# Eight V heads as a 512-wide moving operand, and single rows of 512 for an MLP and an output projection, in a one-token attention kernel

## The chip, the cores and the metric

The kernel runs on one core of one Trainium2 chip. The metric is device time in microseconds (us), the median of several executions of the same program. Five engines work side by side, each in its own program order: PE (TensorE, matrix products), DVE (VectorE), ACT (ScalarE), POOL (GpSimd) and SP, which here only issues the loads. Sixteen DMA engines move the data. In the profile, PEld are PE's weight loads and PEclk is the share of full clock that PE was granted. A line such as `L283` names a line of the kernel's source; the source of the changed kernel has other line numbers.

## The reference

One token decodes through attention over the last 4,096 positions of a cache with 32 heads, and through a small MLP on the same normalised input; the results are multiplied and added to the input. Cut to what matters:

```python
xn = _layernorm(x)                              # x is (1, 1, 512)
q  = xn @ wq                                    # 32 heads of 128
k, v = k_cache[:, :, Sk - W:], v_cache[:, :, Sk - W:]   # W = 4096
scores = einsum("bhqd,bhkd->bhqk", q, k) * Dh ** -0.5
o  = einsum("bhqk,bhkd->bhqd", softmax(scores), v)
s  = o.reshape(B, Sq, 4096) @ wo                # back to 512
# MLP; its shifts leave zeros for a sequence of one token
x1 = xn + hs                                    # hs = shifted @ w2
g  = silu(x1 + gelu(layernorm(x1) @ w3) @ w4)
out = x + s * g
```

Nearly all data are the 32 K and 32 V heads, 1 MB each, every byte used once.

## The kernel before

K and V heads arrive in order through one queue, V five heads behind K. Heads with an even number get their scores on DVE: a multiplication with q (about 2.3 us) and a reduction (4.4 us). Heads with an odd number get them on PE: 32 transposes of 128 x 128, four copies by ACT, and 32 narrow matmuls with q. Four heads share a softmax.

```python
def k_head(h, kn):
    ...
    if h % 2 == 0:                        # DVE
        nc.vector.tensor_tensor(out=prod[:], in0=kn[:], in1=q_bc[...], op=ALU.mult)
        nc.vector.tensor_reduce(out=s["sS"][:, hl // 2, :], in_=prod[:], axis=AX.X, op=ALU.add)
    else:                                 # PE and ACT
        for b in range(NB):
            for i in range(8):
                nc.tensor.transpose(pt[:, i, :], kn[:, b * 8 + i, :], ident_bf[:])
            nc.scalar.copy(out=kt[:, b * 8:(b + 1) * 8, :], in_=pt[:])
    ...
    if hl == G - 1:
        softmax(g)                        # maxima, exponentials: PE, DVE, ACT in turn
```

A V head is used as the stationary operand, 32 weight loads with a matmul of one column after each. The products with the output weights wo, and those of the MLP, go four at a time into rows 0, 32, 64 and 96 of a PSUM tile, 128 wide each:

```python
def rows_add(ps, col, w, last):
    k = col.shape[0]
    for j in range(KC):                   # KC = 4
        nc.tensor.matmul(ps[32 * j:32 * j + 1, :], lhsT=col, rhs=w[0:k, j * P:(j + 1) * P],
                         start=False, stop=last, skip_group_check=True)

def apply_wo(i, ox):                      # once per block of 8 heads
    for t in range(8):
        rows_add(y_ps, ox[:, t:t + 1], wo_blk[i][:, t, :], False)

def v_head(h, v):
    ...
    for c in range(NC):                   # NC = 32
        nc.tensor.matmul(oT[:, k:k + 1], lhsT=v[:, c, :], rhs=s["pT"][:, hl % 2, hl // 2, c:c + 1],
                         start=(c == 0), stop=(c == NC - 1))
    ...                                   # after head 7, 15, 23 and 27:
            ox = repack(i)                # DVE, PE, DVE, DVE
            later.append(lambda: apply_wo(i, ox))
```

The loop `for i in range(H + LAG)` calls `k_head(i)` and then `v_head(i - 5)`. "K27" below is K head 27, "V31" V head 31, the last one. "wo block 0, 1, 2" are the products of heads 0 to 7, 8 to 15 and 16 to 23; the last eight heads have a path of their own, which the change leaves alone.

## Time and profile before

| Kernel before | |
|---|---|
| Time, median of 3 | 197.74 us (197.67 to 197.79) |
| Span of the profiled run | 195.5 us |
| Mean clock granted to PE | 0.649 |
| Last V landed on the first of its DMA engines, on the last | 185.80, 190.54 us |
| PE begins on the last V | 190.58 us, after 1.31 us of waiting |

The prediction below quotes the slices, the waits of the queue and the end of the chain. Three more places matter for what came. The first is part 4 of the page of before, the composition of the chain that ended last:

```profile
DMA 57%; PE 18%; DVE 16%; issue 3%; ACT 3%; SPq 1%; DVEq 0%; ACTq 0%
```

More than half of that chain is transfers: again and again an engine waited for data. The second place is PE's timeline of before from 140 to 156 us. Columns are start, duration, engine, line, operation, output and inputs, shapes and count; in brackets stands the idle time ahead and what ended it.

```profile
140.50 1.03 PE L402 MATMUL oT<-pT,kv 128*128 128x1 bf16 x32
141.87 3.59 PE L283 MATMUL pt<-ident_bf,kv 128*128 128x128 bf16 x32 [0.33 <-DMA kv<-in_A_k_cache_dram]
145.25 0.61 PE L255 MATMUL sT<-qT_bf,kt 128*128 128x1 bf16 x16
146.89 0.99 PE L402 MATMUL oT<-pT,kv 128*128 128x1 bf16 x32 [1.03 <-DVE o L409]
...
149.58 1.01 PE L402 MATMUL oT<-pT,kv 128*128 128x1 bf16 x32 [1.27 <-DMA kv<-in_A_v_cache_dram]
151.99 3.60 PE L283 MATMUL pt<-ident_bf,kv 128*128 128x128 bf16 x32 [1.39 <-DMA kv<-in_A_k_cache_dram]
```

K25 (141.87), a V head and K27 (151.99) all waited for DMA: PE has caught up with the data here. The waits for data add up to 0.33 + 1.27 + 1.39 = 3.0 us. The third place is the same view some 10 us on:

```profile
160.32 1.03 PE L402 MATMUL oT<-pT,kv 128*128 128x1 bf16 x32
166.97 0.21 PE L363 MATMUL ox_ps<-spread,to 128*128 128x64 bf16 x1 [5.61 <-DVE spread L360]
167.79 1.02 PE L139 MATMUL y_ps<-wo,ox 128*1 128x128 bf16 x32 [0.62 <-DVE ox L369]
168.75 2.96 PE L283 MATMUL pt<-ident_bf,kv 128*128 128x128 bf16 x32
```

PE is idle for 5.61 us, the largest gap of the stretch. But this gap doesn't wait for data: it waits for DVE, which stands behind the multiplication and reduction of K28, which stand behind the softmax of heads 24 to 27, which needs the scores of K27. Such a gap moves with K27.

### The profile page before, as it was taken

Reading aid. Unit: us, or ns where it says so; the run is one execution under the profiler, and the core shown is the slowest. Engines: PE = TensorE matmul, PEld = TensorE weight load, DVE = VectorE, ACT = ScalarE, POOL = GpSimd, SP = SyncE. Lnnn points to the kernel's source line nnn. Section 1 sums busy time; section 2 is a strip of 40 time slices with the busy share of each in tenths; the row PEclk is TensorE's granted clock in tenths of the full one; section 3 lists DMA queues with packets and bytes.
Section 4 is the critical chain, followed back from the end, with each engine's and each line's share of the span. In section 5 each row is a group of like instructions: output and inputs, shape, how many; then the busy total and the mean of one; then the engine's idle time right before and its main releaser. Section 6 shows DMA issues by size and latency. Waiting matters only on the chain.

```text
span 195.5 us, 5353 instructions
## 1 busy us (share of the span) xinstructions
PE 125.0 (64%) x2448; PEld 113.4 (58%) x2448; DVE 129.6 (66%) x165; ACT 69.3 (35%) x82; POOL 5.8 (3%) x12
## 2 busy tenths in 40 slices
PE   0564496827969693099783772399584950798663
PEld 0463346827959683099683662299484950687552
DVE  1530059998979988985199919694699559691501
ACT  2003038709345270055453250077170610257000
POOL 2110007000000000000000000000000000000000
PEclk9999999675585555555558585576555555588555
DMA  6999899999999999999999999999999999999970
GB/s 209 409 496 426 372 424 419 424 426 417 426 424 426 426 424 422 422 427 427 422 424 427 422 424 422 427 426 422 422 427 424 424 422 427 429 424 417 418 292 8
DMA packets 11518, 79.18 MB, mean 405 GB/s; under 512 B 1384, under 2 KB 2248, under 8 KB 2504
## 3 DMA queue, kind: packets, MB, share of 16 engines
q1 hardware_dynamic: 11344, 78.85, 96.4%
q8 instruction: 19, 0.31, 0.6%
q10 hardware_dynamic: 152, 0.00, 0.0%
q14 instruction: 3, 0.02, 0.0%
HBM read 78.84 MB, written 0.00 MB: 403 GB/s over the span
## 4 chain that ended last, share of the span: by engine, by line
DMA 57%; PE 18%; DVE 16%; issue 3%; ACT 3%; SPq 1%; DVEq 0%; ACTq 0%
DMA kv<-in_A_v_cache_dram 30%; DMA kv<-in_A_k_cache_dram 18%; DMA wq_sb<-in_A_wq_dram 10%; DVE sS L277 7%; PE pt L283 7%; DVE prod L274 6%; PE oT L402 4%; PE sT L255 2%; ACT kt L284 2%; SPq L76 1%; PE mb_ps L307 1%; PE qT_ps L225 1%; PE qb_ps L234 1%; PE y_ps L139 1%; PE mt_ps L300 1%
## 5 line engine op out<-in xcount | busy, mean ns | idle before, releaser
L284 ACT COPY kt<-pt 128x1024 bf16<-128x1024 bf16 x64 | 60.2, 1026 | 68.2 <-PE pt L283 68.2
L277 DVE TENSOR_REDUCE sS<-prod 128x32 f32<-128x4096 bf16 x16 | 70.6, 4414 | 0.3
L283 PE MATMUL pt<-ident_bf,kv 128*128 128x128 bf16 x512 | 53.4, 298 | 3.4 <-DMA kv<-in_A_k_cache_dram 3.2
L283 PEld LDWEIGHTS <-kv 128*128 128x128 bf16 x512 | 49.8, 141 | 4.7 <-DMA kv<-in_A_k_cache_dram 3.4
L274 DVE TENSOR_TENSOR prod<-kv,q_bc 128x4096 bf16<-128x4096 bf16 x16 | 36.6, 2285 | 6.3 <-DMA kv<-in_A_k_cache_dram 4.1
L402 PEld LDWEIGHTS <-kv 128*128 128x128 bf16 x1024 | 30.6, 102 | 16.5 <-issue 10.0
L402 PE MATMUL oT<-pT,kv 128*128 128x1 bf16 x1024 | 32.6, 165 | 8.3 <-DVE o L409 4.2
L255 PE MATMUL sT<-qT_bf,kt 128*128 128x1 bf16 x512 | 20.4, 166 | 3.5 <-ACT kt L284 3.1
L255 PEld LDWEIGHTS <-kt 128*128 128x128 bf16 x512 | 18.2, 103 | 4.5 <-ACT kt L284 4.2
L297 DVE TENSOR_REDUCE m<-sT 128x2 f32<-128x64 f32 x8 | 1.8, 224 | 19.3 <-PE sT L255 19.3
L139 PEld LDWEIGHTS <-ox 128*1 128x1 bf16 x96 | 2.2, 114 | 19.5 <-DVE ox L369 19.5
L363 PE MATMUL ox_ps<-spread,to 128*128 128x64 bf16 x4 | 0.8, 212 | 17.4 <-DVE spread L360 17.4
L316 ACT ACTIVATE pT<-e 128x128 bf16<-128x128 f32 x8 | 2.5, 310 | 20.7 <-DVE e L312 20.7
L307 PEld LDWEIGHTS mb_ps<-md,ones_f 4*128 4x128 f32 x16 | 3.8, 290 | 6.1 <-DVE md L304 6.1
L307 PE MATMUL mb_ps<-md,ones_f 4*128 4x4 f32 x16 | 4.5, 347 | 4.4 <-DVE md L304 4.4
L322 PE MATMUL den_ps<-pT,ones_bf 128*128 128x128 bf16 x8 | 2.1, 265 | 7.3 <-ACT pT L316 7.2
L300 PE MATMUL mt_ps<-ident_f,m 128*4 128x128 f32 x8 | 2.7, 334 | 5.9 <-DVE m L297 5.9
L236 ACT CAST q_bc<-qb_ps 128x512 bf16<-128x512 f32 x4 | 2.3, 586 | 9.9 <-PE qb_ps L234 9.9
L234 PE MATMUL qb_ps<-wq_sb,xn_rep 128*128 128x512 bf16 x16 | 5.3, 506 | 0.0
L225 PE MATMUL qT_ps<-xn_bf,wq_sb 128*128 128x1 bf16 x64 | 1.9, 165 | 5.2 <-DMA wq_sb<-in_A_wq_dram 5.2
L225 PEld LDWEIGHTS <-wq_sb 128*128 128x128 bf16 x64 | 1.8, 104 | 5.5 <-DMA wq_sb<-in_A_wq_dram 5.5
L309 DVE COPY mb<-mb_ps 128x4 f32<-128x4 f32 x8 | 1.3, 163 | 5.3 <-PE mb_ps L307 5.3
(96 smaller groups left out, 61.6 us busy)
## 6 DMA issues: line engine op xcount, KB each, us to landing
kv<-in_A_k_cache_dram SPq DMA_DIRECT2D x32, 1024.0 KB, 19.6
kv<-in_A_v_cache_dram SPq DMA_DIRECT2D x32, 1024.0 KB, 19.6
wq_sb<-in_A_wq_dram SPq DMA_DIRECT2D x1, 4096.0 KB, 18.9
wo<-in_A_wo_dram SPq DMA_DIRECT2D x3, 1024.0 KB, 20.4
w_sb<-in_B_w_dram SPq DMA_DIRECT2D x1, 1376.0 KB, 6.7
w_sb<-in_B_w_dram SPq DMA_DIRECT2D x1, 1024.0 KB, 8.7
w_sb<-in_B_w_dram SPq DMA_DIRECT2D x1, 512.0 KB
wo_rows<-in_A_wo_dram SPq DMA_DIRECT2D x1, 384.0 KB, 17.5
```

What stands on the lines that cost most here:

```text
L139: nc.tensor.matmul(ps[32 * j:32 * j + 1, :], lhsT=col, rhs=w[0:k, j * P:(j + 1) * P], start=False, stop=last, skip_group_check=True)
L225: nc.tensor.matmul(qT_ps[:, h:h + 1], lhsT=wq_sb[:, c, h * Dh:(h + 1) * Dh], rhs=xn_bf[:, c:c + 1], start=(c == 0), stop=(c == KC - 1))
L234: nc.tensor.matmul(qb_ps[:], lhsT=xn_rep[:, c, :], rhs=wq_h[:, c, 2 * i:2 * i + 8:2, :], start=(c == 0), stop=(c == KC - 1))
L255: nc.tensor.matmul(sT[:, hl // 2, c:c + 1], lhsT=kt[:, c, :], rhs=qT_bf[:, h:h + 1], start=True, stop=True)
L274: nc.vector.tensor_tensor(out=prod[:], in0=kn[:], in1=q_bc[:, h // 2:h // 2 + 1, :].to_broadcast([P, NC, Dh]), op=ALU.mult)
L277: nc.vector.tensor_reduce(out=s["sS"][:, hl // 2, :], in_=prod[:], axis=AX.X, op=ALU.add)
L283: nc.tensor.transpose(pt[:, i, :], kn[:, b * 8 + i, :], ident_bf[:])
L284: nc.scalar.copy(out=kt[:, b * 8:(b + 1) * 8, :], in_=pt[:])
L300: nc.tensor.transpose(mt_ps[:], m1[:].rearrange("p a b -> p (a b)"), ident_f[:])
L307: nc.tensor.matmul(mb_ps[:], lhsT=ones_f[0:G, :], rhs=md[:], start=True, stop=True)
L316: nc.scalar.activation(out=pT[:], in_=e[:], func=ACT.Exp, scale=scale)
L402: nc.tensor.matmul(oT[:, k:k + 1], lhsT=v[:, c, :], rhs=s["pT"][:, hl % 2, hl // 2, c:c + 1], start=(c == 0), stop=(c == NC - 1))
```

## The change

The intent is to send fewer instructions to PE. V heads 4 to 7 and 16 to 19 become the moving operand, 512 wide: 8 matmuls a head with 4 columns of probabilities as weights, into a 128 x 512 tile. ACT copies that tile out, and fp32 matmuls with a selection matrix pick the four useful blocks. The MLP's two rows become one row of 512 (15 matmuls instead of 60), spread afterwards over four rows. The wo blocks 0 to 2 become 8 matmuls each of 512 columns instead of 32 of 128; DVE adds their rows up, and one spread brings the sum into the old accumulator. The diff also moves two small buffers and keeps one buffer of the softmax instead of three; e7 below has these as well and isn't slower. The core of the diff, with cuts marked:

```diff
+MOVED = (1, 4)
 ...
-    hsr_ps = ps_misc.tile([P, P], FP32, tag="misc", name="hsr_ps")
-    rows_open(hsr_ps)
-    for c in range(KC):
-        rows_add(hsr_ps, shifted_bf[:, c:c + 1], w2_sb[:, c, :], c == KC - 1)
 ...
+    hr_ps = ps_misc.tile([1, D], FP32, tag="misc", name="hr_ps")
+    for c in range(KC):
+        nc.tensor.matmul(hr_ps[:], lhsT=shifted_bf[:, c:c + 1], rhs=w2_sb[:, c, :], ...)
+    for i, (m, _) in enumerate(chunks):
+        nc.tensor.matmul(hr_ps[:], lhsT=a_bf[0:m, i:i + 1], rhs=w4_sb[0:m, i, :], ...)
+    hr = wts.tile([1, D], FP32, name="hr")
+    nc.vector.tensor_copy(out=hr[:], in_=hr_ps[:])
     h2_ps = ps_misc.tile([P, P], FP32, tag="misc", name="h2_ps")
     rows_open(h2_ps)
-    for i, (m, _) in enumerate(chunks):
-        rows_add(h2_ps, a_bf[0:m, i:i + 1], w4_sb[:, i, :], i == len(chunks) - 1)
+    rows_add(h2_ps, one_f, hr, True)
 ...
     def apply_wo(i, ox):
+        if i == few_block:
+            ...                          # as before
+            return
+        yr_ps = ps_misc.tile([1, D], FP32, tag="misc", name="yr_ps")
         for t in range(8):
-            rows_add(y_ps, ox[:, t:t + 1], wo_blk[i][:, t, :], False)
+            nc.tensor.matmul(yr_ps[:], lhsT=ox[:, t:t + 1], rhs=wo_blk[i][:, t, :], ...)
+        if i == 0:
+            nc.vector.tensor_copy(out=y_row[:], in_=yr_ps[:])
+        else:
+            nc.vector.tensor_tensor(out=y_row[:], in0=y_row[:], in1=yr_ps[:], op=ALU.add)
+        if i == few_block - 1:
+            rows_add(y_ps, one_f, y_row, False)
 ...
+        if g in MOVED:
+            for c in range(0, NC, 4):
+                nc.tensor.matmul(s["ov"][32 * k:32 * k + 4], lhsT=s["pT"][:, hl % 2, hl // 2, c:c + 4],
+                                 rhs=v[:, c:c + 4, :], start=False, stop=c == NC - 4, ...)
+            if hl == G - 1:
+                nc.scalar.copy(out=ov_sb[:], in_=s["ov"][:])
+                def add(at=h % 8 - 3):
+                    for j in range(4):
+                        nc.tensor.matmul(oT[:], lhsT=ov_sb[:, j, :], rhs=pick_f[:, j, :], ...)
+                    keep(oT, at)
```

## The prediction

> **What bounds the kernel now.** I read the 40 slices first, then who the DMA queue waits for, then the chain that ended last, then the last 10 us, and finally single DMA records of the trace.
>
> The slices (page, part 2) and the first line of part 1:
>
> ```profile
> PE 125.0 (64%) x2448; PEld 113.4 (58%) x2448; DVE 129.6 (66%) x165; ACT 69.3 (35%) x82; POOL 5.8 (3%) x12
> ...
> DMA  6999899999999999999999999999999999999970
> GB/s 209 409 496 426 372 424 419 424 426 417 426 424 426 426 424 422 422 427 427 422 424 427 422 424 422 427 426 422 422 427 424 424 422 427 429 424 417 418 292 8
> ```
>
> No compute engine is over two thirds busy; the DMA engines are full from the second slice to the third from last, at about 424 GB/s. 79.18 MB at 424 GB/s are 186.7 us of the 195.5 us span. The rest is start (some 2 us), a slow last slice, and the tail.
>
> What the queue that issues the loads waits for:
>
> ```profile
> SPq L76 <- DMA kv<-in_A_v_cache_dram: 56.7, 27, 3.5
> SPq L76 <- DMA kv<-in_A_k_cache_dram: 56.4, 29, 2.1
> ...
> SPq L76 <- PE oT L402: 1.8, 3, 1.4
> ```
>
> It waits for older DMAs, not for engines that free buffers. From issue times and the last reader of each buffer I worked out the slack: 23 to 39 us for each reused K buffer; for V 4.1 us (head 7), over 5 us for 8 to 30, 0.03 us for head 31 alone. But head 31 was issued at 173.04 and landed at 190.54, so even that wait is covered by queued transfers. Faster or slower TensorE (PE) in the middle is therefore not worth time by itself.
>
> The end of the chain, and PE there by its timeline:
>
> ```profile
> 173.04 17.50 DMA kv<-in_A_v_cache_dram
> 190.54 0.05 issue
> 190.58 1.01 PE oT L402 x32
> 191.59 0.61 PE y_ps L139 x15
> 192.21 0.02 issue
> 192.23 0.30 DVE y L450
> ```
>
> ```profile
> 188.89 0.38 PE L139 MATMUL y_ps<-wo_rows,o 128*1 128x128 bf16 x8
> 190.58 1.01 PE L402 MATMUL oT<-pT,kv 128*128 128x1 bf16 x32 [1.31 <-DMA kv<-in_A_v_cache_dram]
> ```
>
> The last V lands, then 4.9 us of fixed tail follow. PE had waited only 1.31 us for it. Two things can thus move the end: when that transfer lands, and whether PE is ready then.
>
> The DMA rate in the last stretches, and the queues:
>
> ```profile
> 185.00:187.00 2.00, 1.42 (x44) 1.03 (x44) 0.42 (x2) 0.00 (x0) 0.00 (x0) 0.50 1.00 392
> 187.00:191.00 4.00, 2.44 (x82) 2.08 (x80) 0.32 (x2) 0.00 (x0) 0.00 (x0) 0.50 0.61 230
> ```
>
> ```profile
> q8 instruction: 19, 0.31, 0.6%
> ```
>
> From 187 to 191 only 0.61 of the DMA engines work: some have finished while others lag. The sixteen completions of the last V spread from 185.80 to 190.53 us (offsets: four up to 0.66, two near 2.4, eight from 3.08 to 3.28, one at 3.53, two at 4.63 and 4.73). Early transfers do not: those of wq lie within 0.28 us except one, 1.67 us late. Between them, each of the 19 instruction fetches (16,384 bytes, about 1.05 us, one packet each) makes one more completion about 1.6 us late; after the ninth (98.4 us) one completion is 3.3 us late for the first time, after the seventeenth (177.9) one is 4.8 us late. I read this as fetches going round eight of the sixteen engines, each costing its engine some 1.6 us of data. The slowest engine then sets the landing: three fetches on two engines.
>
> **What the Trainium skill says.** "Runtime: NRT & Kernel Launch", Instruction fetch mechanics: instruction memory is refilled in 16 KiB blocks of 256 instructions by the sequencer's own DMA queue. The trace agrees: fetch n starts when PE has started 256 n instructions, give or take the queue depth (n = 3 at 46.1 us: 768; n = 17: 4,328 against 4,352). "DMA: Bandwidth & Descriptors", Why a DMA increments its semaphore by 16: each participating engine adds one when its part is done, only all sixteen mean landed; this is what the spread shows. Its Specifications give a ceiling of 435 GB/s; 424 here is near it, so bytes leave nothing to gain. "TensorE: Matmul & The Clock Gate", Back-to-back issue gap: N / 1.2 GHz cold, so 427 ns for N = 512. The trace agrees: the weight loads of the 512-wide q matmuls come every 0.42 us until the clock warms at 27.5 us, and 0.2 us after.
>
> **The change, part by part.** Pairs of weight load and matmul (fp32 ones count two passes, as in the 16 records for 8 calls of line 307):
>
> - Removed: 17 pairs for the MLP's w2 row, 44 for w4, 96 for three wo blocks, 8 x 32 = 256 for eight V heads. Sum 413.
> - Added: 15 (MLP row), 8 and 8 (two row spreads in fp32), 24 (wo rows), 2 (zero openings), 64 (V heads), 16 (picks). Sum 137.
>
> Net -276 pairs, -552 instructions. PE has 4,903 records with its seven sequencer ones, so 4,351 remain: one below 17 x 256 = 4,352. Fetch 17 falls at or past the end; fetch 16 (at 4,096, 255 before the end) comes at about 186 us, and leaves each of the eight engines with two. The late completions at 4.63 and 4.73 should fall to about 3.2; then the 3.53 one is last. The last V lands at 185.80 + 3.5 = 189.3 instead of 190.5: **-1.2 us**. The bytes saved, 3 x 16 KB, are 0.1 us of all engines, contained in this.
>
> PE time. A V head took 1.0 us in 32 pairs; eight 512-wide matmuls take 3.4 us cold, 1.7 us warm: +0.7 to +2.4 us for each of eight heads. In 60 to 80 us PE is busy 13.3 of 20, so +9.7 cold would be more than the 6.7 idle, but V buffers there have 4 to 10 us slack, and 512-wide streams should warm the clock, which also shortens the transposes (0.3 us each now). Heads 16 to 19 run at 130 to 142, and PE waits for data again by 150. Both hidden. The MLP row costs 15 x 0.43 = 6.4 us instead of some 1.3, from 15.3 on, plus copy and spread, so ends near 23 against wq's landing at 22.3; q may start 1 us later but on a warmer clock, and the queue has data to 37. Hidden. The wo blocks cost 8 x 0.43 = 3.4 us against 1.02. Two are hidden; the third, at 167.8 us, stands in the last busy stretch.
>
> That stretch: +2.4 us at 167.8; the warm clock on K head 29's transposes and gaps at 173 and 175 give back perhaps 0.9; then the copies of K 29 and 31 (0.94 us each by ACT) pace PE. So the last softmax, and V 28 to 30, come about 1.5 us later, and PE is ready for the last V at 189.27 + 1.5 = 190.8 instead of 190.58: **+0.2 us**, if the instruction order stays. Separate fp32 spread passes could add another 1.
>
> **Rivals.**
>
> 1. *DMA floor*: the last V lands at 189.3 and PE is ready. 197.74 - 1.2 = 196.5 us. For: the instruction count lands just under a page limit. Against: PE's present readiness, 189.27, leaves no slack.
> 2. *PE takes the end*: the wo row of block 2 shifts the last softmax by 1.5 to 2.5 us. 197.9 to 198.9. For: the chain of PE from 167 to 187 has few gaps. Against: the order of the instructions may differ, and moved groups free their accumulator by an ACT copy instead of a DVE multiply that sat behind a 4.4 us reduction.
> 3. *Nothing moves*: the spread comes from something else than fetches (the two wo_few loads, of 16 partitions, also appear to load some engines by 2.4 us), the last V lands as before. 197.7. Against: the step in lateness follows each fetch.
> 4. *PE backlog in the middle starves the queue*: over 200 us. Against: 10 us and more of slack almost everywhere.
>
> **Range and chances.** I give rival 1 about half, 2 about a third, 3 the rest. The middle of that is 197.0 us; 8 in 10 between 196.2 and 198.5. A gain over 2% (below 193.8) has no room: bytes alone need 186.7 us, and start and tail are unchanged. A loss over 2% needs rival 4.
>
> **What would show it.** Fetches on the PE instruction queue 16 or 17 instead of 19; the last V's slowest completion near 3.5 us behind its fastest, landing near 189.3. PE's wait before the last V: near zero if I am right about readiness; still over 1 us if PE has more room than I think; none, with V 31 begun well after landing, for rival 2. The third wo row at 3.4 us cold. GB/s unchanged in the middle slices. The prediction fails if fetches do not fall, if lateness stays at 4.7 with fewer of them, or if slices in the middle drop below 420.

## The result, and the profile after

| | Before | After |
|---|---|---|
| Time, median (range, runs) | 197.77 us (197.67 to 198.76, 6) | 204.52 us (201.92 to 204.80, 6) |
| Span of the profiled run | 195.5 us | 200.1 us |
| Mean clock granted to PE | 0.649 | 0.759 |
| PE records, instruction fetches | 4,903, 19 | 4,353, 17 |
| Last V landed, on its last DMA engine | 190.54 us | 189.44 us |
| PE begins on the last V | 190.58 us | 195.20 us |

The ratio is 1.0316 (1.0266 to 1.0367): slower by 3.2%. A run is slow when it is over 1.5% above the fastest of its kernel; ratios compare fast runs alone, of the same rounds, so they aren't quite the ratios of the medians. The profiled run of after was its fastest, 201.92 us, so the traces show 4.6 us of span of a loss that is mostly nearer 7 us; where the rest comes from is told under the runs e14 and e15.

The page of after, parts 1 to 4:

```profile
PE 139.6 (70%) x2172; PEld 105.4 (53%) x2172; DVE 131.8 (66%) x169; ACT 70.5 (35%) x84; POOL 5.8 (3%) x12
...
DMA  6999999999999999999999999999999999999800
GB/s 202 407 479 419 398 418 421 424 429 419 428 423 424 423 424 429 421 426 429 421 428 424 421 424 423 424 428 428 423 429 426 424 419 429 429 423 420 331 6 3
...
q8 instruction: 17, 0.28, 0.6%
...
PE 38%; DVE 34%; ACT 16%; issue 8%; DMA 2%; POOL 1%; ACTq 0%; DVEq 0%; POOLq 0%
```

The slices look healthy until one sees the two at the end: DMA ran at its full rate and was done early, and then stood still while the engines worked on. The chain says it outright. Transfers are 2% of it, where they were 57%; PE, DVE and ACT hand work to each other from the MLP to the end, without one wait for data. There are fewer PE instructions, by 276 pairs, and PE is busy for 14.6 us more.

The end of that chain in after, with start and duration first:

```profile
185.80 0.22 DVE m L308
186.20 0.39 PE mt_ps L312
...
188.48 0.32 ACT pT L328
...
195.25 0.94 PE oT L459 x32
196.20 0.56 PE y_ps L141 x9
196.78 0.30 DVE y L505
```

The last V had landed at 189.44. Nothing here waits for it: PE comes to it from other V heads at 195.2, because the last softmax (its last maximum at 185.93, against 180.05) was 5.9 us later than before.

PE's timeline of after, the stretch shown above for before:

```profile
126.05 1.87 PE L401 MATMUL yr_ps<-wo,ox 128*1 128x512 bf16 x4 [0.62 <-DVE ox L381]
...
132.44 1.89 PE L443 MATMUL ov<-kv,pT 128*4 128x512 bf16 x8
...
145.38 3.25 PE L443 MATMUL ov<-kv,pT 128*4 128x512 bf16 x8
149.30 1.05 PE L453 MATMUL oT<-pick_f,ov_sb 128*128 128x4 f32 x8 [0.68 <-ACT ov_sb L448]
150.22 1.50 PE L295 MATMUL pt<-ident_bf,kv 128*128 128x128 bf16 x24
...
155.80 2.51 PE L295 MATMUL pt<-ident_bf,kv 128*128 128x128 bf16 x22
...
170.64 0.21 PE L375 MATMUL ox_ps<-spread,to 128*128 128x64 bf16 x1 [5.62 <-DVE spread L372]
171.47 1.87 PE L401 MATMUL yr_ps<-wo,ox 128*1 128x512 bf16 x4 [0.61 <-DVE ox L381]
173.27 2.55 PE L295 MATMUL pt<-ident_bf,kv 128*128 128x128 bf16 x24
```

K25 begins at 150.22 instead of 141.87, K27 at 155.80 instead of 151.99, and neither waits for data. The gap of 5.6 us for DVE's `spread` is there as before, only later, and K29 follows at 173.27 instead of 168.75. So the loss is made between 126 and 156 us, kept by the gap, and added to by the wo row at 171.47.

What the issuing queue waits for in after, two of its lines:

```profile
SPq L77 <- DMA kv<-in_A_v_cache_dram: 53.1, 26, 2.1
...
SPq L77 <- PE oT L459: 0.2, 1, 0.2
```

It still waits for transfers and hardly ever for PE to free a buffer. The loads were not starved.

### The profile page after: what moved, and what is told of

Same layout as the page of the kernel before. It is cut to its first block, busy times and chain, and to the rows that moved or that the text cites. A ratio compares the mean times of both kernels' runs of the same rounds, so it can differ in the third digit from the quotient of the medians.

```text
span 200.1 us, 4811 instructions
## 1 busy us (share of the span) xinstructions
PE 139.6 (70%) x2172; PEld 105.4 (53%) x2172; DVE 131.8 (66%) x169; ACT 70.5 (35%) x84; POOL 5.8 (3%) x12
## 4 chain that ended last, share of the span: by engine, by line
PE 38%; DVE 34%; ACT 16%; issue 8%; DMA 2%; POOL 1%; ACTq 0%; DVEq 0%; POOLq 0%
ACT kt L296 15%; DVE sS L289 14%; DVE prod L286 10%; PE ov L443 7%; PE pt L295 6%; PE oT L459 5%; PE yr_ps L401 5%; PE sT L261 3%; DMA x_bf<-in_A_x_dram 2%; PE mb_ps L319 2%; DVE e L324 2%; PE hr_ps L214 1%; PE a_ps L203 1%; PE mt_ps L312 1%; DVE mx L314 1%
## 5 line engine op out<-in xcount | busy, mean ns | idle before, releaser
L295 PE MATMUL pt<-ident_bf,kv 128*128 128x128 bf16 x512 | 47.6, 272 | 1.6 <-ACT kt L296 1.3
L295 PEld LDWEIGHTS <-kv 128*128 128x128 bf16 x512 | 43.4, 127 | 7.2 <-issue 6.2
L459 PEld LDWEIGHTS <-kv 128*128 128x128 bf16 x768 | 22.5, 100 | 8.4 <-issue 8.3
L459 PE MATMUL oT<-pT,kv 128*128 128x1 bf16 x768 | 24.1, 164 | 1.8 <-DVE o L436 1.5
L261 PE MATMUL sT<-qT_bf,kt 128*128 128x1 bf16 x512 | 19.9, 165 | 5.1 <-ACT kt L296 4.2
L261 PEld LDWEIGHTS <-kt 128*128 128x128 bf16 x512 | 16.9, 98 | 8.9 <-ACT kt L296 7.4
L443 PE MATMUL ov<-kv,pT 128*4 128x512 bf16 x64 | 17.7, 427 | 0.0
L443 PEld LDWEIGHTS <-pT 128*4 128x4 bf16 x64 | 5.3, 92 | 12.9 <-issue 8.2
L406 DVE TENSOR_TENSOR y_row<-y_row,yr_ps 1x512 f32<-1x512 f32 x2 | 1.3, 674 | 15.6 <-PE yr_ps L401 15.6
L401 PE MATMUL yr_ps<-wo,ox 128*1 128x512 bf16 x24 | 10.2, 539 | 1.8 <-DVE ox L381 1.8
L217 DVE COPY hr<-hr_ps 1x512 f32<-1x512 f32 x1 | 0.7, 678 | 7.8 <-PE hr_ps L214 7.8
```

Of the source, the lines that this page charges most:

```text
L261: nc.tensor.matmul(sT[:, hl // 2, c:c + 1], lhsT=kt[:, c, :], rhs=qT_bf[:, h:h + 1], start=True, stop=True)
L401: nc.tensor.matmul(yr_ps[:], lhsT=ox[:, t:t + 1], rhs=wo_blk[i][:, t, :], start=(t == 0), stop=(t == 7))
L443: nc.tensor.matmul(s["ov"][32 * k:32 * k + 4], lhsT=s["pT"][:, hl % 2, hl // 2, c:c + 4], rhs=v[:, c:c + 4, :], start=False, stop=c == NC - 4,
```

## The experiments

The expectations speak of theory A and of rivals under other letters. **Theory A**: PE's own added work, first in the stretch from 126 to 156 us (V heads 16 to 19 wide, and the wo row of block 1) and then in the wo row of block 2, makes the last softmax late. **Theory C**: other parts cost too, such as the MLP row, the first wo rows or wide heads anywhere. **Theory D**: the changed kernel is bound by PE and DVE from the first multiplication to the end. The chief **rival** (B, or B2, where a text names it so: the wo rows): DVE, which works in order, waits for PE's wo rows to add them up. In after two such additions stand ahead of the multiplication of K22 and of K30, and DVE is idle for 15.6 us ahead of them. A further question came up on the way, why the same program's runs fall into two kinds some 2 us apart.

To read all traces in one way I took four moments from each: when PE begins the transposes of K27; when it is ready for the last V (it begins on it, less its wait just before); the difference; and when the last V landed on its last engine. All in us; the times are those of the fast runs, and "row" or "rows" tells how wo block 2 is done, as one row of 512 or in four rows.

| Run | K27 | Ready | Difference | Landed | wo block 2 | Times |
|---|---|---|---|---|---|---|
| before | 151.99 | 189.27 | 37.3 | 190.54 | rows | 197.7 |
| after | 155.80 | 195.20 | 39.4 | 189.44 | row | 201.92 to 204.80 |
| e1_after_again | 156.19 | 195.62 | 39.4 | 189.72 | row | 202.57 to 204.71 |
| e2_group1_only | 154.32 | 193.85 | 39.5 | 189.47 | row | 198.79 to 200.75 |
| e3_wo2_rows | 159.61 | 196.57 | 37.0 | 189.46 | rows | 201.68 to 203.51 |
| e4_group1_wo2_rows | 152.42 | 189.16 | 36.7 | 189.80 | rows | 197.41 to 198.67 |
| e5_mlp_groups123 | 152.88 | 189.56 | 36.7 | 189.32 | rows | 196.60 to 197.98 |
| e6_groups123_alone | 153.95 | 190.84 | 36.9 | 189.49 | rows | 197.22 to 200.13 |
| e7_mlp_alone | 153.34 | 190.47 | 37.1 | 191.96 | rows | 197.52 to 198.72 |
| e8_mlp_wo_rows | 152.19 | 191.40 | 39.2 | 190.65 | row | 198.21 to 198.66 |
| e9_row_by_act | 158.23 | 197.80 | 39.6 | 189.42 | row | 200.79, 202.39 |
| e10_q_rows_first | 152.95 | 192.43 | 39.5 | 189.48 | row | 199.36 to 202.03 |
| e11_groups123_q_rows_first | 153.38 | 190.16 | 36.8 | 189.74 | rows | 196.29 to 197.76 |
| e12_wide_alone | 154.88 | 191.85 | 37.0 | 189.69 | rows | 198.13 to 198.78 |
| e13_wo1_rows | 154.61 | 194.04 | 39.4 | 189.49 | row | 199.30 to 201.98 |
| e14_after_look | 155.94 | 195.33 | 39.4 | 189.25 | row | 202.05 |
| e15_after_look | 157.84 | 197.25 | 39.4 | 189.62 | row | 204.09 |

The trace of e9 fell in a run that is slow (204.46 us), so it is used for its order and its waits, and its moments with care. The kernel before ran beside each batch, at medians of 197.77 to 197.89 us. At the 2% from which a verdict is given, e1 is slower, e3, e9 and e13 are unclear, e14 and e15 are single runs without one, and the others are the same as before; smaller differences below rest on the intervals and the traces.

The column of differences is the main finding. From K27 to readiness is a nearly fixed chain in these seventeen traces: 36.7 to 37.3 us in the kernels that do wo block 2 in four rows, 39.2 to 39.6 in those that do it in one row. It doesn't depend on when K27 began (152 to 160), on the way of the V heads, or on the MLP. The end is the later of landing and readiness, plus the tail. So two questions decide everything: when does K27 begin, and is there a wide wo row after it.

### The change again, and its parts in the late stretch taken back

e1 is the changed kernel unchanged, to see its spread.

> The changed kernel once more, for a second trace. Of its first runs one (the one whose trace is kept) took 201.9 us and the others 204.1 to 204.8. Theory A and theory B (below) say nothing of which comes; I expect most runs at 204 to 205. If the trace is of such a run, it should show where a further 2.7 us go: I expect the same chain (last softmax late, PE late for the last V, last V landed near 189.4), only later, not a DMA that is slower.

It took 203.87 us (202.57 to 204.71), ratio 1.0287 (1.0232 to 1.0342). The loss repeats, and so does the spread.

e2 gives heads 16 to 19 the old form:

```diff
-MOVED = (1, 4)
+MOVED = (1,)
```

> V heads 16 to 19 back as 32 narrow pairs each; the rest of the change stays. In the changed kernel the maximum over scores of the last group is taken at 185.9 us against 180.05 before. Theory A: 3.8 us of these 5.9 are PE's backlog from heads 16 to 19 (K head 27's transposes start at 155.8 against 152.0), so this one's stands near 182.1, PE is ready for the last V near 191.4, span near 196.3, time about 198.5 us. Theory B (all of it is the third wo row, whose add on DVE waited 7.0 us for PE and held K head 30's multiply): nothing is regained, 201 to 204 us.

It took 200.61 us, ratio 1.0097 (1.0035 to 1.0159): about two thirds of the loss gone. That lies between theory A's 198.5 and theory B's 201 or more; one run of the four took 198.79, the others 200.54 to 200.75. K27 begins at 154.32 although this trace is of the later of the two kinds (below), and 39.5 us follow as in after.

e3 gives wo block 2 the old form, and spreads the sum of blocks 0 and 1 after block 1:

```diff
-        if i == few_block:
+        if i >= 2:
 ...
-        if i == few_block - 1:
+        if i == 1:
```

> The third wo block (heads 16 to 23) back as rows of 128 into y; heads 16 to 19 stay wide. Theory A: 2.1 us are regained, last maximum near 183.9, time about 200 us (202 if the slower kind of run). Theory B: all is regained, 196.5 to 197.7 us.

It took 201.77 us, ratio 1.0207 (1.0154 to 1.0260). The difference fell from 39.4 to 37.0 us: the wide row of block 2 costs 2.4 us on the path, a little more than the 2.1 that I had taken from the two traces. Yet its trace ends no earlier than that of after. It is of the later kind, and its K27 began at 159.61, 1.8 us later still than in e15, the trace of after of that kind: K25's transposes took 3.5 us instead of 2.1 and the picks just before them 1.87 instead of 1.06, at a lower clock. Judged by times alone, the run would have been misread.

e4 takes both back:

```diff
-MOVED = (1, 4)
+MOVED = (1,)
 ...
-        if i == few_block:
+        if i >= 2:
 ...
-        if i == few_block - 1:
+        if i == 1:
```

> Both undone; MLP row, wo rows of blocks 0 and 1 and wide V heads 4 to 7 stay. Both theories: last maximum near 180.1 us, PE ready near 189.3. About 4,573 PE instructions, so fetch 17 comes some 220 instructions before the end, near 186 us: the last V lands between 189.4 and 190.5; time 196.5 to 197.7 us. A third theory C (the MLP row or the first wo blocks also cost) would show 198 us or more.

It took 198.01 us (197.41 to 198.67), ratio 0.9997 (0.9956 to 1.0039). The expectation had given 198 us or more to theory C, and the median is just there, but against the runs of before beside it nothing is left of the loss, with the MLP row, heads 4 to 7 wide and two wo rows still in place. K27 begins at 152.42, PE is ready at 189.16 and waits again for the last V. The earlier landing (189.80) gave nothing back in this trace, since the next transfer, of wo rows, was held up:

```profile
189.85 1.02 PE L459 MATMUL oT<-pT,kv 128*128 128x1 bf16 x32 [0.69 <-DMA kv<-in_A_v_cache_dram]
191.59 0.60 PE L141 MATMUL y_ps<-wo_rows,o 128*1 128x128 bf16 x16 [0.72 <-DMA wo_rows<-in_A_wo_dram]
```

An instruction fetch began at 189.0 us; I take it that it fell on this transfer instead of on the last V. e4 is the run that supports theory A best: what it takes back is PE's added work from 130 us on, and with it DVE's second wait for a row. DVE's first wait, for the row of block 1, is still there, at 7.9 us, and the loss is gone all the same.

### Each part by itself

e5 and e6 ask whether wide V heads are harmful as such. e5 has twelve of them, heads 4 to 15, all before the late stretch, with the MLP row and no wo row; e6 the same with the old MLP.

```diff
-MOVED = (1, 4)
+MOVED = (1, 2, 3)
 ...
     def apply_wo(i, ox):
-        if i == few_block:
-            for t in range(8):
-                rows_add(y_ps, ox[:, t:t + 1], wo_blk[i][:, t, :], False)
-            return
+        for t in range(8):
+            rows_add(y_ps, ox[:, t:t + 1], wo_blk[i][:, t, :], False)
+        return
```

> A version meant to keep the gain of fewer fetches without lateness at the end: MLP row kept, V heads 4 to 15 wide, no wo rows at all. About 4,305 PE instructions by my count, so no fetch 17 before the end. Theory A (lateness of PE comes from wide heads near the end and from wo rows, and lateness up to 120 us is made good by 160): last V lands near 189.5, PE ready near 189.3, time 196.3 to 196.9 us. Theory C (any wide head's lateness is carried to the end): 199 us or more.

> The same with the MLP as before: about 4,381 PE instructions, fetch 17 some 30 before the end, after the last V. Theory A: 196.3 to 196.9 us. It also shows whether the MLP row itself decides between two kinds of runs (K head 0's multiply at 25.5 us in two traces of the changed kernel, at 27.3 in two others, with the clock halved from 24 to 27.5 us in the latter): if so this one has one kind only, its multiply near 26.6 as before, all runs within 0.5 us.

e5 took 197.44 us, ratio 0.9968 (0.9940 to 0.9995); a sixth run, slow, isn't counted. e6 took 198.32, ratio 1.0035 (0.9987 to 1.0082), with runs from 197.22 to 200.13. Both are above the 196.3 to 196.9 that was expected, and e6's runs aren't within 0.5 us of each other: a spread of 2.9 us is there without the MLP row, and I leave it open. So twelve early wide heads as such don't bring the loss, but they use up nearly all the slack: PE waits for no K or V data between 40 us and K27 in either trace, and K27 is 0.9 us late in e5 and 2.0 in e6. At the end of e5 PE and data meet: the last V landed at 189.32 and PE began on it at 189.56, as soon as its own order allowed. Here the earlier landing is used.

e7 is the MLP row alone, e8 the MLP row and the three wo rows without wide V heads. Against after, e7 has `MOVED = ()` and the `apply_wo` of e5, e8 only `MOVED = ()`.

> The MLP row alone. Theory A: costs and gains nothing at the end: 4,827 PE instructions, fetch 17 before the last V as in the kernel before: last V lands near 190.5, 197.5 to 197.9 us. If the late kind of start (2 us) were carried to the end even here, some runs would be at 199 us.

> The three wo rows (and the MLP row, which alone changed nothing), no wide V head. Theory A: what they leave at the end is the third row's own time, some 2 us at the last maximum (near 182 us), so 198 to 199 us in the early kind of run. Theory B (the wo rows are the loss): 201 us or more.

e7 took 198.03 us, ratio 0.9997 (0.9968 to 1.0027): nothing. In its trace the first of the DMA engines was already 1.3 us later with wq than in before (21.98 against 20.65), and so it was with the last V (187.05 against 185.80), which landed at 191.96; that is a matter of the transfers, in the first 22 us, which I leave open. e8 took 198.54, ratio 1.0034 (1.0022 to 1.0047). Its PE timeline shows the wo row of block 2 on the path:

```profile
152.19 3.57 PE L295 MATMUL pt<-ident_bf,kv 128*128 128x128 bf16 x32
...
167.14 0.21 PE L375 MATMUL ox_ps<-spread,to 128*128 128x64 bf16 x1 [5.62 <-DVE spread L372]
167.97 1.86 PE L401 MATMUL yr_ps<-wo,ox 128*1 128x512 bf16 x4 [0.62 <-DVE ox L381]
169.77 2.26 PE L295 MATMUL pt<-ident_bf,kv 128*128 128x128 bf16 x24
```

K27 begins on time, so the wo row of block 1 alone does no harm. The comparison with e2, which has wide heads 4 to 7 as well, shows that these aren't always hidden. Both traces are of the later kind, with the first multiplication at 27.5 and 27.3 us; the one of K12 then begins at 76.2 in e8 and at 78.6 in e2, and K27 at 152.19 and 154.32. With the late start e2 has no slack left for the four heads, and its median is 2 us above e8's. In e8 PE is ready at 191.40, 39.2 us after K27: 2.1 us later than in before, for data that landed at 190.65. As K27's data aren't there before about 152, by these traces a kernel with a wide row in block 2 isn't ready before some 152.0 + 39.2 = 191.2 us (an estimate). The 1.1 us that the fewer fetches gain are out of its reach.

e12 is the reverse, the eight wide V heads with the old MLP and old wo products: after with the parts of the diff for the MLP and `apply_wo` taken back.

> Wide V heads 4 to 7 and 16 to 19 alone; MLP and wo as in the kernel before. Theory A: 3 to 4 us at the last maximum (near 183.5 us): 199.5 to 200.5 us. Theory B: 196.5 to 197.7 us. With e8 the two parts should add up to the whole, 4 to 6 us.

It took 198.40 us, ratio 1.0031 (1.0018 to 1.0044), less than theory A had said and more than theory B. K27 begins at 154.88, 2.9 us late, and PE is ready at 191.85, 37.0 us later. Each part alone costs only 0.6 to 0.8 us of time, though it makes PE late by 2.1 us (e8) and 2.6 us (e12) at the end: before had 1.3 us of waiting to spare. In the whole change the two add up, 2.1 + 2.6 = 4.7 of the 5.9 us by which readiness moved from 189.27 to 195.20, and the spare is used once.

e13 asks for the remaining 1.2 us. It gives wo block 1 the old form, since its row falls between 126 and 134 us just ahead of wide heads 16 to 19:

```diff
-        if i == few_block:
+        if i in (1, few_block):
```

> The whole change, but the second wo block (applied at 126 us) as rows of 128. If the excess over the parts' sum comes from this row meeting wide heads 16 to 19, the readiness of PE for the last V falls back to the sum of the parts, 189.3 + 2.1 + 2.6 = 194.0 us, and the time to 200.7 us in the early kind. If the excess is of another origin: 201.9 us and more.

Its three fast runs took 199.30 to 201.98 us, ratio 1.0137 (1.0050 to 1.0225); a fourth, 202.61, is slow. PE was ready at 194.04, but that this is the expected 194.0 is luck: the trace is of the later kind. Against e15, the trace of after of that kind, the two stand at the same place just before the row (127.11 and 127.14), and K27 begins 3.2 us earlier (154.61 against 157.84). Some 1.4 us of that are V19's eight matmuls, which took 1.89 us here and 3.30 in e15, by the clock granted to them; whether the row brought that about isn't shown. The rest, some 1.8 us, is the row's when heads 16 to 19 follow it; without them it cost nothing (e8).

### The rival: DVE's wait for the rows

e9 takes the additions away from DVE. ACT copies each wo row, and PE spreads each at once:

```diff
-        if i == 0:
-            nc.vector.tensor_copy(out=y_row[:], in_=yr_ps[:])
-        else:
-            nc.vector.tensor_tensor(out=y_row[:], in0=y_row[:], in1=yr_ps[:], op=ALU.add)
-        if i == few_block - 1:
-            rows_add(y_ps, one_f, y_row, False)
+        nc.scalar.copy(out=y_row[:], in_=yr_ps[:])
+        rows_add(y_ps, one_f, y_row, False)
```

> The whole change, but ACT instead of DVE takes each wo row out of PSUM, and PE spreads each at once (16 more pairs). DVE's waits for these rows (8.6 and 7.0 us in the changed kernel) are gone. Theory B2 (the waits on DVE are what costs): last maximum back to 181 to 182 us, 198.5 us. Theory A (PE's own time costs, DVE is only just as late): the last maximum moves under 1.5 us, 201 to 204 us.

The two fast runs took 200.79 and 202.39 us, ratio 1.0186 (1.0142 to 1.0230), far from theory B2's 198.5; two more, 204.46 and 206.20, are slow. The wait of DVE in after, by its timeline, and the same place in e9:

```profile
134.58 0.67 DVE L406 TENSOR_TENSOR y_row<-y_row,yr_ps 1x512 f32<-1x512 f32 x1 [8.59 <-PE yr_ps L401]
135.19 2.27 DVE L286 TENSOR_TENSOR prod<-kv,q_bc 128x4096 bf16<-128x4096 bf16 x1
```

```profile
127.31 2.29 DVE L286 TENSOR_TENSOR prod<-kv,q_bc 128x4096 bf16<-128x4096 bf16 x1 [0.69 <-DMA kv<-in_A_k_cache_dram]
```

The multiplication of K22 begins at 127.31 instead of 135.19, and its wait is for data. So the edit did what it was to do. But K25 began no earlier (152.3, against 150.2 in after), and from K27 to readiness it was 39.6 us again. In part this trace had a lower clock (V19 took 3.58 us, K25's transposes 3.5), so the traces of after and e4 have to settle what is left. The first of the two waits isn't on the chain that ended last in after, and e4 keeps it without a loss. The second is on the chain:

```profile
178.08 0.32 PE yr_ps L401
178.43 0.68 DVE y_row L406
179.10 2.21 DVE prod L286
181.34 4.43 DVE sS L289
185.80 0.22 DVE m L308
```

PE's timeline shows how much it is worth:

```profile
185.01 0.35 PE L261 MATMUL sT<-qT_bf,kt 128*128 128x1 bf16 x8 [0.34 <-ACT kt L296]
186.20 0.37 PE L312 MATMUL mt_ps<-ident_f,m 128*4 128x128 f32 x1 [0.83 <-DVE m L309]
```

PE's last scores were done at 185.36, DVE's at 185.76. PE then waited 0.83 us for the maximum, against 0.32 at this place in before and e9. So of the 15.6 us of idle DVE, the most striking new line of the profile, about 0.5 us make the end late (an estimate from these two traces and before's); without them PE's scores would end last.

### The two kinds of runs

e14 and e15 are the changed kernel again, one look each, to catch a trace of each kind.

> The changed kernel, one look. If its time is over 203.5 us, theory D says: first multiply near 27.3 us instead of 25.5, the clock halved from about 24 to 27.5 us, and all later steps late by that 1.8 us. If instead the first multiply is at 25.5, the lateness begins later and the trace shows where.

> The changed kernel again, one look more, with the same expectations as the look before it: a second chance of a trace of the slower kind.

They took 202.05 and 204.09 us, one of each kind. The traces part early. PE's timeline in after, the early kind, for the q products of 128 x 1 and of 512 columns:

```profile
22.12 1.74 PE L231 MATMUL qT_ps<-xn_bf,wq_sb 128*128 128x1 bf16 x64 [0.41 <-DVE bv L222]
23.72 3.61 PE L240 MATMUL qb_ps<-wq_sb,xn_rep 128*128 128x512 bf16 x16
```

And in e15, the late kind:

```profile
23.08 1.79 PE L231 MATMUL qT_ps<-xn_bf,wq_sb 128*128 128x1 bf16 x64 [0.41 <-DVE bv L222]
24.73 4.91 PE L240 MATMUL qb_ps<-wq_sb,xn_rep 128*128 128x512 bf16 x16
```

In e15 PE begins 1.0 us later and takes 1.3 us longer for the same 16 matmuls; the trace has the clock at half from 24.0 us. The 1.0 us comes from the MLP row just before, whose 11 products with w4 took 4.24 us in e15 and 3.13 in after. In after the full clock was granted from 18.5 us for 13.7 us; in e15 from 20.6 us, for 3.4. All twelve traces that have the MLP row and the old order of q fall in line: six with the full clock from 18.5 to 19.2 us begin the first multiplication at 25.4 to 25.6 us, six with it from 20.4 to 21.2 us at 27.2 to 27.5. What sets the moment I haven't found. The first multiplication of a K head, which needs these, starts at 27.3 us instead of 25.4. From there the delay is carried to the end: K27 at 157.84 instead of 155.80 in after, readiness 197.25 instead of 195.20. A kernel whose chain is unbroken from the start to the end has no wait for data in which such a delay could vanish. A kernel that still has slack loses it: e8 also began late (27.5 us), and its K27 is at 152.19.

e10 removes that dependence in part by doing the 512-wide q products first, ahead of the narrow ones (the seven lines of the `qT_ps` block move below the loop that fills `q_bc`).

> The whole change, with the 512-wide q matmuls moved ahead of the 64 narrow ones, so that DVE's first multiply starts about 2 us earlier and the clock has a dense stretch as soon as wq is there. Theory D (the changed kernel is bound by PE and DVE from the first multiply to the end, and its two kinds of runs come from the clock at q): first multiply near 23.5 to 24.5 us in all runs, time 0.5 to 2 us lower, 200 to 202 us, and the kinds closer together. If the kinds come from elsewhere: spread as before, up to 204.8 us.

The three fast runs took 199.36 to 202.03 us, ratio 1.0133 (1.0088 to 1.0178); a fourth, 203.01, is slow. The first multiplication starts at 23.7 us, K27 at 152.95, and 39.5 us follow. So more than half of the loss goes. But K27 is 2.85 us earlier than in after, for a start 1.7 us earlier, and that start wasn't simply handed on: V4's eight matmuls took 3.30 us (1.89 in after), and the multiplication of K20 came only 0.4 us earlier (117.6 against 118.0); then V19's took 1.89 us (3.25 in after). The clock that the wide heads happen to be granted moves K27 as much as the start does. The spread of some 3 us stays, so the two kinds didn't come closer together.

### A version that beats both

e11 joins what had been found: e5 (wide heads 4 to 15, the MLP row, wo products as before) with the order of e10.

> Candidate: MLP row, V heads 4 to 15 wide, no wo rows, and the wide q matmuls first. e5 without the last took 196.6 to 198.0 us in fast runs, with PE ready 0.2 us after the last V landed. Theory D: the same or up to 0.5 us faster and steadier: 196.3 to 197.2 us. Otherwise no different from e5.

It took 196.85 us (196.29 to 197.76, six runs), against 197.82 for before, ratio 0.9958 (0.9936 to 0.9979). The last V landed at 189.74 and PE began on it at 190.16. This is the fastest. It is 0.4% ahead of before, clear of noise; from e5 it can't be told apart, the intervals overlap.

## Why the prediction was wrong

The prediction was 197.0 us, within 196.2 to 198.5, and it left a loss over 2% to rival 4 alone. Its steps in turn:

1. **Instruction fetches and the landing: right.** It said 4,351 PE records, at most 17 fetches, and a last landing at 189.3. The trace has 4,353, 17 and 189.44, even though V31 was issued 5 us later than before (178.11 against 173.04). The lag between first and last engine fell from 4.73 to 3.55 us. Fetch 16 came at 190.0 us, after that landing and not near 186, because PE was late; that isn't why the landing was early, since the last V of e2, with fetch 16 at 186.2, landed at 189.47. (Of the completions that the prediction lists, those from 3.08 to 3.28 are seven, not eight.) But landing no longer set the end.

2. **"Faster or slower TensorE (PE) in the middle is therefore not worth time by itself": the step that failed.** It was derived from the slack of the buffers, that is, from whether a late PE would delay loads. It wouldn't, and didn't: rival 4, a starved queue, is refuted by the slices and by the 0.2 us above. What a late PE delays is the softmax, then DVE's next K head behind it, then PE itself behind DVE, and so on: the fixed 37 us from K27 to the end. The prediction checked one way by which lateness reaches the end and took it for the only one.

3. **"Heads 16 to 19 run at 130 to 142, and PE waits for data again by 150. Both hidden": half wrong.** Heads 4 to 7 were hidden in the trace of after: with the wo row of block 0 they made K17 3.5 us late, and K19 only 0.4. After a late start they weren't (e2 against e8). Heads 16 to 19 were not; at 150.22 PE was just beginning K25 and never waited for K or V data again. The price of a head was well estimated, +0.7 to +2.4 us: three took 1.89 instead of about 1.0, the fourth, with the granted clock at 0.57, 3.25. What was missing was the sum for this stretch, which the prediction had done for 60 to 80 us only. It can be done from the two timelines. Wide heads with opening and picks: 3 x 1.89 + 3.25 + 0.39 + 1.05 = 10.4 us against 4.0, so +6.4. The wo row of block 1: 1.87 + 0.58 + 0.59 + 0.38 = 3.4 against 1.0, so +2.4. Faster transposes of K21, K23 and K25 on the warmer clock: 3.4 + 2.1 + 2.1 against 3.5 + 2.9 + 3.6, so -2.4. In all about +6.4 us, into 3.0 us of waits for data. K27 was 3.8 us late. e12 and e13 agree with both terms, though part of e13's is V19's clock.

4. **The wo rows: price right, place half right.** 3.4 us instead of 1.02 each, as said. "Two are hidden" holds for block 0, and for block 1 only without the wide heads (e8, e13).

5. **The third wo row, "+1.5" and PE "ready for the last V at 189.27 + 1.5 = 190.8": mis-sized.** e8 measures the sum as 191.40, so +2.1; against the kernels with four rows it is 39.4 - 37.0 = 2.4, the raw cost. The 0.9 us that warmer transposes were to give back didn't come: K29's weren't faster (3.2 us against 3.0), and K31's were (2.1 against 3.35), but the last maximum then waited for DVE.

6. **The MLP row "hidden": right for the row alone.** e7's ratio is 0.9997. In the trace of after the first multiplication began at 25.4 us, before's at 26.6; in the later kind it begins at 27.3, and in after there is no slack in which that could vanish.

7. **Rival 2, PE takes the end: right in kind, too small.** It allowed for a shift of 1.5 to 2.5 us, the third wo row alone; the shift was 5.9, of which 3.8 were already there at K27 and about 2.1 came from that row. Its chance of a third was too low because step 2 had ruled out the larger term.

8. **What it hadn't seen at all**: DVE's additions (15.6 us of idle DVE, of which about 0.5 us count at the end), and the spread of 2 to 3 us between runs of one program, which comes once the chain has no wait for data left. By their times, most runs of after are of the late kind, hence 204.5 instead of 202.

## What to carry to other kernels

Ask of every gap what ends it: a wait for a transfer absorbs a delay, a wait for another engine passes it on, and a profile with plenty of idle time can have almost no slack. Before adding work to an engine that is "only two thirds busy", sum the added time against its waits for data in that very stretch, up to the point where it must be back on time. Where the same instruction-saving form can be placed early or late, place it where waits for data still follow (heads 4 to 15 here, not 16 to 19), and watch the run-to-run spread: the changed kernel, which ends on a compute chain, spread over 2 to 3 us with the clock it was granted.

## What the Trainium skill lacked or had wrong

- "Runtime: NRT & Kernel Launch", Instruction fetch mechanics, calls the cost of crossing a block boundary "mostly hidden". For the engine's sequencer that may be so, but in this kernel, bound by transfers, the completions read as if each fetch also held up one DMA engine, and so the last transfer: in before the last V's landing was spread over 4.73 us, in after over 3.55, and it landed 1.1 us earlier. What counts is how many fetches come before it: in the three traces whose seventeenth began before 187 us (before, e7, e8) the spread is 4.70 to 4.92 us, in the fourteen others 3.22 to 3.92. The page says nothing of this cost, nor of which DMA engines carry the fetches.
- "TensorE: Matmul & The Clock Gate", Part 4: PE-mode transpose, says that the full clock doesn't engage for transposes. Here it does once other work has warmed PE: 24 transposes took 1.50 us in after at 150.22, with the granted clock at 1.00, and 32 took 3.59 us in before at 141.87, with it at 0.50, so 62 against 112 ns each. What agrees is that transposes by themselves didn't warm it: K27 in before took 3.60 us with the granted clock at 0.50.
- The same page, Part 1: The HAM clock gate, says that the phase of the clock's window varies from run to run and that the penalty is under 1% of a typical span, so not to be modelled. Here e14 and e15, the same program, differ by 2.0 us, 1.0%; the q products took 3.61 us in after and 4.91 in e15, and the chain carried the delay to the end. The two kinds part with the moment at which the full clock is first granted (18.5 us in after, 20.6 in e15); I haven't shown that the window's phase is what sets it.
- No page that I used tells how to find slack: that idle time which waits for an engine, like the 5.6 us for DVE in both kernels, isn't slack, and only waits for data are (3.0 us ahead of K27 in before).
